# Order of the SyncE transfers where the forward convolution ends and the MLP begins

## The chip, the cores and the metric

One Trainium2 chip, of which one core is used. The metric is the device time of one execution in microseconds (us), the median of the runs. Five engines work side by side: TensorE (PE; PEld is its weight load), VectorE (DVE), ScalarE (ACT), GpSimd (POOL) and SyncE (SP), which here only issues DMA transfers. Each engine works through its own list of instructions in order. Transfers move data between the chip's DRAM and its on-chip memory on 16 DMA engines, which SP's and POOL's transfers share.

## The reference

Four residual layers on x of shape 2048 x 512 (bf16), convolution and MLP in turn, and the gradients of all inputs and weights for a given `grad_out`:

```
x = x + A(layernorm(x))        # A(q) = q * (conv(kv, ssm_k) + kv * ssm_D),  kv = shift_conv(k) * v
x = x + B(layernorm(x))        # B(x) = gelu(x w1 + b1) w2 + b2,  w1 512 x 1376
x = x + A(layernorm(x))
x = x + B(layernorm(x))
outputs: x, and d/d(q, k, v, shift_k, ssm_k, ssm_D, w1, b1, w2, b2) of <x, grad_out>
```

The bracket in A does not depend on x, so the kernel computes it once, as `y`, and uses it in both A layers. The long convolution is done by a real Fourier transform of length 4096, as matmuls with tables of cosines and sines.

## The kernel before, in words

`ssm_kernel` runs three stages: `phase_conv_forward` (which makes y), `phase_mlp` (all four layers forward, and the backward pass of the MLPs) and the backward convolution together with the weight gradients. The change is at the end of the first stage and at the start of the second.

**End of the forward convolution.** The spectrum is cut into five groups, 0 to 4. For each group `spectrum(g)` is TensorE's transform of kv, evicted by ScalarE into a tile `KVg`; `multiply(g)` is VectorE's product of `KVg` with the spectrum of the filter (tiles `pr_t`, `pr_u`, result `Yg`, or `y_res` for group 3); `inverse(g)` is TensorE's back transform (`iv_ps`), evicted by ScalarE into `W[m]`, m = 0, 1. The filter's spectrum lies in DRAM (`Hspec_d`); `load_spec(g)` fetches a group of it. Groups 2 and 4 share one buffer, `Hg`, so `load_spec(4)` waits until `multiply(2)` has read it for the last time; `multiply(4)` waits for `load_spec(4)`. `store_spec(g)` writes `KVg` to DRAM for the backward stage.

In the same stretch q is normalised for the first layer. Its four slices of 512 rows, `qs[0]` to `qs[3]`, lie in the memory that the MLP weights take over afterwards: slices 0 and 1 under `w1`, slices 2 and 3 under `w2` (both have the name `w_sb` in the profile). When a slice is normalised, POOL stores it to DRAM (`n_d<-w_sb`). `start_weights(..., 0)` loads w1 and `start_weights(..., 1)` loads w2 (rows 0 to 1279, then the last 96) and the bias b2 as one more row of w2's tile. So a weight's load waits for POOL's stores out of the memory that it overwrites. `load_x(s)` brings slice s of the residual x into `x_sl` by two transfers, and `y_res<-n_d` brings normalised slices 0 and 1 back.

After `multiply(4)` VectorE runs `even()` (tiles `ib` and `W`), then `res.w.finish()`, one small instruction that scales the row b2 (`w_sb<-w_sb`), then `block0` (`ibx`, `W`, `y_res`), which gives the first rows of y, and `first_sum`, the first residual sum with its statistics (`rstd`, `nmr`). From these ScalarE makes the normalised rows for the first MLP (`low<-x_sl,nmr,rstd`), SP turns them by DMA transposes (`low<-low`), and TensorE multiplies them with w1 (`mm_ps<-low,w_sb`). Before that TensorE makes turned copies of both weights (`oo_ps<-ident,w_sb`, `oo_ps<-w_centre,w_sb`, evicted into `w2T_sb` and `w1T_sb`); the very first of these reads the last chunk of w2, with the scaled row b2 in it. VectorE meanwhile works through the rest of the back transform (`others`, `outs`) and the sums of the next rows, and blocks of 256 rows follow one another through both MLPs.

**What sets the order.** In the convolution each engine's list is the order in which the code calls its operations. In the MLP it is the list of numbers `SEQUENCE`, by which `Plan.listed` takes the planned steps. `flip_rows` copies `grad_out` with rows of each second half block reversed from DRAM to DRAM (`goB_d`, 1024 rows of 1 KB); it is read much later by the backward pass of the MLP.

Of the kernel before, what the change touches and what calls it, by code (L numbers as in the profile page):

```python
# [195 lines left out]
def flip_rows(out, src2d, first, eng, n=256):  # L196
    rs = src2d.ap[0][0]
    eng.dma_start(out=out, in_=bass.AP(tensor=src2d.tensor, offset=src2d.offset + first * rs,
                                           ap=[[512 * rs, out.shape[0]], [-rs, n], [1, src2d.shape[1]]]))
# [8 lines left out]
def tok_io(nc, sb, ap2d, flipped, i, store=False, eng=None):  # L208
    eng = eng or nc.sync
    lo = ap2d[i * 512:i * 512 + 256, :].rearrange("(t p) d -> p t d", p=P)  # L210
    hi = flipped[i].rearrange("(t p) d -> p t d", p=P)
    for s, d in ((sb[:, 0:2, :], lo), (sb[:, 2:4, :], hi)):
        last = eng.dma_start(out=d, in_=s) if store else eng.dma_start(out=s, in_=d)
    return last
# [628 lines left out]
def phase_conv_forward(ctx, nc, tc, dims, consts, dram, res, aps):  # L843
# [4 lines left out]
    nc = Ordered(nc, tc, ("tensor", "vector", "scalar", "gpsimd", "sync"))  # L848
# [26 lines left out]
    order = p.listed(OPEN_SEQUENCE, start, dict(OPEN_FREE))  # L875
    b_ = Slots(Ordered(nc.nc, tc, ("tensor", "vector", "scalar", "gpsimd", "sync")), tiles, p.held, None)
# [45 lines left out]
    def store_spec(g):  # L922
        lo, src = (0, KVpair[0]) if g == 1 else (GROUPS[g][1], KVs[g])
        nc.sync.dma_start(out=dram.KVspec[:, :, lo:lo + 4, :], in_=src)

    def load_x(s):
        tok_io(nc, res.x[:, s * TS:(s + 1) * TS, :], aps["A_q"].flatten_outer_dims(), dram.qB, s)
# [37 lines left out]
    for g in (3, 4):  # L965
        sts.append(fk.streams(GROUPS[g][0], spare[g - 3]))
    tmp = [foldp.tile([P, 2, 2, 2, 512], BF16, name=f"ib{x}", tag=("fold_s", "fold_d")[x], bufs=1) for x in range(2)]
    start_weights(nc, res.w, dims, aps, 0)
    res.x = res.xpool.tile([P, NT, D], BF16, name="x_sl", tag="fold_x", bufs=1)
    spectrum(3, lambda: normalise("scalar"))  # L970
    multiply(2)
    load_spec(4)
    load_x(0)
    nc.sync.dma_start(out=ns[0], in_=tok(dram.n[0], 0))
    store_spec(3)
    spectrum(4, lambda: normalise("scalar"))
    res.low = [shared(res, "low", i) for i in range(len(SHARED))]
    load_x(1)
    nc.sync.dma_start(out=ns[1], in_=tok(dram.n[0], 1))
    start_weights(nc, res.w, dims, aps, 1)  # L980
    store_spec(4)
    for s in (2, 3):
        load_x(s)
    inverse(2)
    multiply(3)
    inverse(3)
# [3 lines left out]
    for m in range(2):  # L990
        ib[m].even()
    res.w.finish()
    flip_rows(dram.goB, aps["grad_out"].flatten_outer_dims(), 511, nc.sync)
    inverse(4)
    yv = res.y[:, :, :].rearrange("p (i h) d -> p i h d", i=4)
    px = foldp.tile([P, 2, 2, 2, 512], BF16, name="ibx", tag="fold_t", bufs=2)
# [330 lines left out]
def start_weights(nc, w, dims, aps, part):  # L1327
    D, F, ND, NFC = dims.D, dims.F, dims.ND, dims.NFC
    FP = NFC * P
    nfull = F // P  # L1330
    rem = F - nfull * P
    assert rem == 96
    w1_ap, w2_ap = aps["B_w1"], aps["B_w2"]
    if part == 0:
        nc.sync.dma_start(out=w.w1[:, :, 0:F], in_=w1_ap.rearrange("(c p) f -> p c f", p=P))
        nc.gpsimd.memset(w.w1[:, :, F:FP], 0.0)
        nc.gpsimd.memset(w.centre, -1.0 / D)
        return
    nc.gpsimd.memset(w.w2[rem:P, nfull, :], 0.0)
    nc.sync.dma_start(out=w.w2[:, 0:nfull, :], in_=w2_ap[0:nfull * P, :].rearrange("(c p) d -> p c d", p=P))  # L1340
    nc.sync.dma_start(out=w.w2[0:rem, nfull, :], in_=w2_ap[nfull * P:F, :])
    nc.sync.dma_start(out=w.w2[rem:rem + 1, nfull, :], in_=aps["B_b2"].rearrange("(o d) -> o d", o=1))

    def finish():
        b2 = w.w2[rem:rem + 1, nfull, :]
        nc.vector.tensor_scalar(out=b2, in0=b2, scalar1=1.0 / PAD_H, scalar2=None, op0=ALU.mult)

    w.finish = finish
# [6 lines left out]
def tok(ap2d, s):  # L1355
    return ap2d[s * 512:(s + 1) * 512, :].rearrange("(t p) d -> p t d", p=P)
# [822 lines left out]
LATE = {}  # L2179
SEAM = 9.0  # L2180
READY = {0: -5.0, 1: 0.5, 2: -5.0, 3: -5.0, -1: -12.0, -2: -12.0}
FREE = {"PE": -12.0, "ACT": -10.8, "DVE": -3.4, "POOL": 0.4, "SP": -10.0}
SEQUENCE = (
# [132 lines left out]
@with_exitstack  # L2316
def phase_mlp(ctx, nc, tc, dims, consts, dram, res, aps):
    S, D, F, NT, ND, NFC = dims.S, dims.D, dims.F, dims.NT, dims.ND, dims.NFC
    go_ap = aps["grad_out"].flatten_outer_dims()
    out0 = aps["out_0"].flatten_outer_dims()  # L2320
    out1 = aps["out_1"].flatten_outer_dims()
    m = Mid()
    m.D, m.ND, m.NFC = D, ND, NFC
    m.sum_on_act = False
    m.ident, m.ones_f = consts.ident, consts.onescol_f
    m.x, m.y, m.rstd, m.nmr, m.mhalf = res.x, res.y, res.rstd, res.nmr, res.mhalf
    m.st, m.mv, m.tail = res.st, res.mv, res.tail
    m.n_d, m.h_d, m.gz_d, m.gp_d = dram.n, dram.h, dram.gz, dram.gp
    with ExitStack() as st:
        lanes = st.enter_context(tc.tile_pool(name="m_l", bufs=1, reuse_waits="tile"))  # L2330
        psum = st.enter_context(tc.tile_pool(name="m_ps", bufs=1, space=bass.MemoryType.PSUM, reuse_waits="tile"))
        m.w = res.w
        w, tiles = m.w, {k: [] for k in SIZES}

        w.w2T = lanes.tile([P, ND, NFC * P], BF16, name="w2T_sb")
        w.w1T = lanes.tile([P, NFC, D], BF16, name="w1T_sb")
        low = [res.low[i][:, x * 1024:x * 1024 + 1024] for i in (1, 2, 3) for x in range(2)]
        tiles["n"], tiles["nT"] = low[0:4], low[4:6]

        def slots(tag, n):  # L2340
            for _ in range(n):
                i = len(tiles[tag])
                tiles[tag].append(lanes.tile([P, SIZES[tag]], BF16, name=f"l_{tag}_{i}"))

        for tag, k in (("g", 4), ("h", 1), ("n", 4), ("u", 2)):
            slots(tag, k)
        big, small, rest = [], [], []
        for t in res.old:
            k = t.shape[-1] // 4096
            big += [t[:, 2816 * i:2816 * i + 2816] for i in range(k)]  # L2350
            small += [t[:, 2816 * k + 1024 * i:2816 * k + 1024 * i + 1024] for i in range(k)]
            rest.append(t[:, 3840 * k:4096 * k])
        tiles["g"] += big[0:4]
        tiles["h"] += [big[7]] + big[4:7]
        tiles["nT"] += [*small[0:2], small[7]]
        tiles["gx"], tiles["g1"] = small[2:6], [small[6]]
        junk = [rest[1]]
        tiles["dg"] = [rest[3 + i // 2][:, P * (i % 2):P * (i % 2) + P] for i in range(4)]
        m.cols = rest[2].bitcast(F32).rearrange("p (a t) -> p a t", a=8)
        w.b1col = rest[5][:, 0:2 * NFC].bitcast(F32)  # L2360
        tiles["mm"] = [psum.tile([P, 512], F32, name=f"mm_ps{i}") for i in range(SLOTS["mm"])]
        tiles["oo"] = [psum.tile([P, 512], F32, name=f"oo_ps{i}") for i in range(SLOTS["oo"])]

        def forward_done(b_):
            res.wstack.close()
            gp_ = res.gystack.enter_context(tc.tile_pool(name="gres", bufs=1, side="right"))
            G3 = gp_.tile([P, NT, D], BF16, name="G3")
            gypool = res.gystack.enter_context(tc.tile_pool(name="gypool", bufs=1, side="right"))
            m.gy = res.gy_bf = gypool.tile([P, NT, D], BF16, name="gy_bf")
            m.G = [G3, res.x]  # L2370

        p = Plan(SLOTS)

        def load_g(b_, x):
            s, e = x // 2, x % 2
            src = dram.goB[s] if e else go_ap[s * 512:s * 512 + HB, :]
            b_.nc.sync.dma_start(out=m.G[0][:, 2 * x:2 * x + 2, :], in_=src.rearrange("(t p) d -> p t d", p=P))

        m.early, m.behind = {}, []

        def early(b_, k):
            m.early[k] = shared(res, "dw_tm", k)[:, :].rearrange("p (t f) -> p t f", t=NT)
            which, i, c = weight_grad_units(NFC)[k]
            b_.nc.sync.dma_start_transpose(out=m.early[k], in_=m.h_d[(3, 1)[i]][:, c, :])

        p = mlp_plan(m, consts, dram, go_ap, out0, out1, aps["B_b1"], forward_done, load_g, early)
        order = p.listed(SEQUENCE, lambda o: READY.get(o.blk, 1.0), dict(FREE))
        b_ = Slots(Ordered(nc, tc, ("tensor", "vector", "scalar", "gpsimd", "sync")), tiles, p.held, junk)
        fill = busy_fill(order, p.held)
        for o in order:  # L2390
            if o in fill:
                (tag, i), n = fill[o]
                keep_busy(b_.nc, consts, tiles[tag][i][:, 0:256], n)
            o.fn(b_)
    return m


# [63 lines left out]
```

## Time and profile before

| | |
|---|---|
| median of 3 runs | 772.45 us (771.81, 772.45, 776.12) |
| profiled execution, its own time | 779.16 us |
| its span | 777.4 us |
| TensorE, VectorE, ScalarE, GpSimd busy | 95%, 92%, 75%, 30% of the span |
| granted clock of TensorE, mean | 0.993 |
| DMA, mean over the span | 220 GB/s |

The profile is of one execution, whose time stands beside its span. Its times are counted from the start of the span. The page gives each engine's busy time and the chain of work that ended last; the queries used here are the waits (who waited for whom), the timeline (instructions of one engine in order of time, neighbours of one kind merged), the windows (busy time, granted clock and DMA traffic of a stretch) and the DMA issues with their time to landing. The change moves transfers that are issued between 108 and 156 us of the span.

### The profile page before, as it was taken

Reading aid. Unit: us, or ns where it says so; the run is one execution under the profiler, and the core shown is the slowest. Engines: PE = TensorE matmul, PEld = TensorE weight load, DVE = VectorE, ACT = ScalarE, POOL = GpSimd, SP = SyncE. Lnnn points to the kernel's source line nnn. Section 1 sums busy time; section 2 is a strip of 40 time slices with the busy share of each in tenths; the row PEclk is TensorE's granted clock in tenths of the full one; section 3 lists DMA queues with packets and bytes.
Section 4 is the critical chain, followed back from the end, with each engine's and each line's share of the span. In section 5 each row is a group of like instructions: output and inputs, shape, how many; then the busy total and the mean of one; then the engine's idle time right before and its main releaser. Section 6 shows DMA issues by size and latency. Waiting matters only on the chain. (4 is left out here: it accounts for less than half of the span.)

```text
span 777.4 us, 13662 instructions
## 1 busy us (share of the span) xinstructions
PE 740.9 (95%) x5167; PEld 453.5 (58%) x5167; DVE 713.4 (92%) x1154; ACT 580.7 (75%) x788; POOL 234.8 (30%) x308
## 2 busy tenths in 40 slices
PE   8999897879999999999999999989999999999996
PEld 6765343566566666767566566534444456567764
DVE  8997987899999999999999998993999998999972
ACT  5999895689999999999888865445323169986761
POOL 4534960002224426434425342220012223020110
PEclk9999999999999999999999999999999999999998
DMA  9878769614655457569779879999999997844561
GB/s 316 313 287 310 268 234 379 139 41 141 174 160 146 123 134 202 181 170 256 179 217 257 216 205 232 217 251 323 264 274 261 318 369 259 312 113 168 160 183 44
DMA packets 205528, 170.96 MB, mean 220 GB/s; under 512 B 100435, under 2 KB 185110, under 8 KB 205334
## 3 DMA queue, kind: packets, MB, share of 16 engines
q1 hardware_dynamic: 192246, 128.88, 59.9%
q0 software_dynamic: 13216, 41.20, 14.6%
q8 instruction: 40, 0.66, 0.3%
q14 instruction: 26, 0.21, 0.1%
HBM read 76.36 MB, written 76.36 MB: 196 GB/s over the span
## 5 line engine op out<-in xcount | busy, mean ns | idle before, releaser
L56 PEld LDWEIGHTS <-w_sb 128*128 128x128 bf16 x903 | 85.9, 99 | 39.8 <-DMA low<-low 5.2
L56 PEld LDWEIGHTS <-dw_tm 128*128 128x128 bf16 x672 | 63.3, 98 | 64.1 <-issue 0.3
L56 PE MATMUL mm_ps<-low,w_sb 128*128 128x256 bf16 x660 | 88.3, 276 | 3.7 <-DMA low<-low 3.7
L56 PE MATMUL dw_ps<-G,dw_tm 128*128 128x512 bf16 x336 | 83.1, 379 | 0.0
L56 PE MATMUL dw_ps<-x_sl,dw_tm 128*128 128x512 bf16 x336 | 80.2, 379 | 0.0
L56 PEld LDWEIGHTS <-w2T_sb 128*128 128x128 bf16 x704 | 68.8, 98 | 16.4 <-issue 1.0
L56 POOL TENSOR_TENSOR rstd<-rstd,mhalf 128x2 f32<-128x2 f32 (+1 forms) x28 | 36.3, 1296 | 104.8 <-DVE rstd L56 103.5
L56 POOL TENSOR_SCALAR ibx<-ident,ib 128x128 bf16<-128x128 bf16 x32 | 33.4, 1044 | 84.5 <-DVE W L56 82.1
L56 PE MATMUL mm_ps<-W,w2T_sb 128*128 128x256 bf16 x440 | 58.3, 272 | 0.5 <-ACT l_g L56 0.3
L56 ACT ACTIVATE l_g<-l_g 128x2816 bf16<-128x2816 bf16 x22 | 57.3, 2604 | 1.4 <-DVE l_g L56 1.2
L2149 ACT ACTIVATE dw_o<-dw_ps 128x512 bf16<-128x512 f32 x21 | 12.5, 594 | 49.9 <-PE dw_ps L56 38.1
L2039 ACT ACTIVATE dw_tm<-dw_tp 128x1024 bf16<-128x1024 bf16 x38 | 38.9, 1024 | 9.9 <-PE dw_tp L56 9.5
L56 DVE SCALAR_TENSOR_TENSOR gw_junk<-gy_bf,kTc 128x1024 bf16<-128x1024 bf16 x32 | 39.2, 1225 | 2.9 <-ACT gy_bf L1176 1.3
L56 PEld LDWEIGHTS <-ib 128*128 128x128 bf16 x264 | 25.6, 98 | 27.8 <-DVE ib L56 1.0
L56 ACT ACTIVATE l_n<-l_n,ib 128x512 bf16<-128x512 bf16 x32 | 25.5, 828 | 13.5 <-POOL ib L56 8.2
L56 PE MATMUL oo_ps<-w1T_sb,ib 128*128 128x512 bf16 x154 | 35.0, 379 | 0.0
L56 ACT ACTIVATE low<-x_sl,nmr,rstd 128x512 bf16<-128x512 bf16 x36 | 30.3, 873 | 5.4 <-DVE nmr L56 5.4
L56 PE MATMUL mm_ps<-lane_t,w2T_sb 128*128 128x256 bf16 x264 | 34.0, 273 | 0.0
L56 ACT ACTIVATE W<-W 128x2816 bf16<-128x2816 bf16 x12 | 31.8, 2647 | 0.0
L56 ACT ACTIVATE ibx<-mm_ps 128x512 bf16<-128x512 f32 (+1 forms) x36 | 20.4, 580 | 14.2 <-PE mm_ps L56 14.1
L56 DVE TENSOR_TENSOR l_g<-l_g,l_g 128x2816 bf16<-128x2816 bf16 x19 | 30.7, 1613 | 0.0
L56 PE MATMUL oo_ps<-w_sb,l_h 128*128 128x512 bf16 x132 | 30.4, 379 | 0.0
(381 smaller groups left out, 1973.7 us busy)
## 6 DMA issues: line engine op xcount, KB each, us to landing
dw_fm<-gz_d SPq DMA_DIRECT2D x22, 512.0 KB, 8.8
l_n<-n_d SPq DMA_DIRECT2D x26, 256.0 KB, 4.1
gz_d<-ib SPq DMA_DIRECT2D x7, 704.0 KB, 5.1
W<-gp_d SPq DMA_DIRECT2D x7, 704.0 KB
n_d<-low SPq DMA_DIRECT2D x18, 256.0 KB, 2.6
h_d<-l_h SPq DMA_DIRECT2D x6, 704.0 KB
gz_d<-ibx SPq DMA_DIRECT2D x6, 704.0 KB, 4.4
KVspec_d<-KVg SPq DMA_DIRECT2D x4, 1024.0 KB
```

The costliest lines, as they stand in the source:

```text
L56: return self.tc.keep_in_program_order(f(*args, **kwargs))
L2039: nc.scalar.activation(out=dst, in_=ps, func=ACT.Identity)
L2149: nc.scalar.activation(out=o, in_=ps, func=ACT.Identity)
```

## The change

Nothing is added to the computation and nothing is left out; SP issues the same transfers in another order. The load of w1 moves behind `load_spec(4)`, the first slice of x and the first normalised slice; the loads of x slices 2 and 3 move ahead of w2; b2 is issued ahead of w2 instead of behind it; and the flipped copy of `grad_out` is issued inside the MLP, after the eighth of SP's planned steps, instead of ahead of the MLP.

```diff
@@ phase_conv_forward
-    start_weights(nc, res.w, dims, aps, 0)
     res.x = res.xpool.tile([P, NT, D], BF16, name="x_sl", tag="fold_x", bufs=1)
     spectrum(3, lambda: normalise("scalar"))
     multiply(2)
     load_spec(4)
     load_x(0)
     nc.sync.dma_start(out=ns[0], in_=tok(dram.n[0], 0))
+    start_weights(nc, res.w, dims, aps, 0)
     store_spec(3)
     spectrum(4, lambda: normalise("scalar"))
     res.low = [shared(res, "low", i) for i in range(len(SHARED))]
     load_x(1)
     nc.sync.dma_start(out=ns[1], in_=tok(dram.n[0], 1))
+    for s in (2, 3):
+        load_x(s)
     start_weights(nc, res.w, dims, aps, 1)
     store_spec(4)
-    for s in (2, 3):
-        load_x(s)
     inverse(2)
...
     res.w.finish()
-    flip_rows(dram.goB, aps["grad_out"].flatten_outer_dims(), 511, nc.sync)
     inverse(4)
@@ start_weights, part 1
     nc.gpsimd.memset(w.w2[rem:P, nfull, :], 0.0)
+    nc.sync.dma_start(out=w.w2[rem:rem + 1, nfull, :], in_=aps["B_b2"].rearrange("(o d) -> o d", o=1))
     nc.sync.dma_start(out=w.w2[:, 0:nfull, :], in_=w2_ap[0:nfull * P, :].rearrange("(c p) d -> p c d", p=P))
     nc.sync.dma_start(out=w.w2[0:rem, nfull, :], in_=w2_ap[nfull * P:F, :])
-    nc.sync.dma_start(out=w.w2[rem:rem + 1, nfull, :], in_=aps["B_b2"].rearrange("(o d) -> o d", o=1))
@@ phase_mlp
+FLIP_AFTER = 7
...
+        flip_after = [o for o in order if o.eng == "SP"][FLIP_AFTER]
         for o in order:
...
             o.fn(b_)
+            if o is flip_after:
+                flip_rows(dram.goB, go_ap, 511, b_.nc.sync)
```

The lists of TensorE, VectorE and ScalarE stay as they were; SP's changes at three places, and on POOL the third store of a normalised slice now stands ahead of the clearing of w1's spare columns.

The first place is SP's list where `multiply(2)` ends. Before (`w_sb<-in_B_w_dram 128x4x1376` is w1, `Hg` the spectrum of group 4):

```order
L56 DMA KVspec_d<-KVg 256x1x2048
L56 DMA w_sb<-in_B_w_dram 128x4x1376
L56 DMA Hg_1482<-Hspec_d 128x2x2048
L56 DMA x_sl<-in_A_q_dram 128x2x512
L56 DMA x_sl<-qB_d 128x2x512
L56 DMA y_res<-n_d 128x4x512
```

and now:

```order
L56 DMA KVspec_d<-KVg 256x1x2048
L56 DMA Hg_1479<-Hspec_d 128x2x2048
L56 DMA x_sl<-in_A_q_dram 128x2x512
L56 DMA x_sl<-qB_d 128x2x512
L56 DMA y_res<-n_d 128x4x512
L56 DMA w_sb<-in_B_w_dram 128x4x1376
```

w1 went from ahead of these four loads to behind them.

The second place is SP's list around w2 (`w_sb<-in_B_w_dram 128x10x512` and `96x512`; `w_sb<-in_B_b_dram` is b2). Before, from the second normalised slice on:

```order
L56 DMA y_res<-n_d 128x4x512
L56 DMA w_sb<-in_B_w_dram 128x10x512
L56 DMA w_sb<-in_B_w_dram 96x512
L56 DMA w_sb<-in_B_b_dram 1x512
L56 DMA KVspec_d<-KVg 256x1x2048
L56 DMA x_sl<-in_A_q_dram 128x2x512
L56 DMA x_sl<-qB_d 128x2x512
...
L56 DMA low<-in_B_b_dram 1x5x128 x2
```

and now:

```order
L56 DMA y_res<-n_d 128x4x512
L56 DMA x_sl<-in_A_q_dram 128x2x512
L56 DMA x_sl<-qB_d 128x2x512
...
L56 DMA w_sb<-in_B_b_dram 1x512
L56 DMA w_sb<-in_B_w_dram 128x10x512
L56 DMA w_sb<-in_B_w_dram 96x512
L56 DMA KVspec_d<-KVg 256x1x2048
L56 DMA low<-in_B_b_dram 1x5x128 x2
```

The four loads of x slices 2 and 3 went ahead of w2, and b2 stands first of the three.

The third place is SP's list at the start of the MLP. Before:

```order
L56 DMA low<-in_B_b_dram 1x96
L56 DMA goB_d<-in_grad_out_dram 1024x1x512
L56 DMA_TRANSPOSE low<-low 128x4x128 x2
L56 DMA low<-n_d 128x2x512 x2
L56 DMA_TRANSPOSE lane_t<-in_grad_out_dram 128x4x128
```

and now:

```order
L56 DMA low<-in_B_b_dram 1x96
L56 DMA_TRANSPOSE low<-low 128x4x128 x2
L56 DMA low<-n_d 128x2x512 x2
L56 DMA_TRANSPOSE lane_t<-in_grad_out_dram 128x4x128
L56 DMA_TRANSPOSE low<-low 128x4x128 x2
L56 DMA_TRANSPOSE lane_t<-in_grad_out_dram 128x4x128
L56 DMA goB_d<-in_grad_out_dram 1024x1x512
```

The flipped copy went from ahead of the first block's transposes to behind the second pair of them.

## Rows read from the trace of the kernel before

**Rows 1.** The chain that ended last, its first piece: start us, us, what

```profile
481.28 0.36 DVE x_sl L56
```

**Rows 2.** Waits of VectorE, 100 to 175 us: total us, times, longest us

```profile
DVE pr_t L56 <- DMA Hg<-Hspec_d: 6.6, 1, 6.6
DVE nmr L56 <- POOL rstd L56: 1.7, 2, 0.9
```

**Rows 3.** Timeline of VectorE: start us, us, instruction, count [idle before, who ended it]

```profile
104.70 1.28 DVE L56 TENSOR_TENSOR pr_u<-KVg,Hg 128x1024 bf16<-128x1024 bf16 x2
...
113.60 0.68 DVE L56 TENSOR_TENSOR y_res<-pr_u 128x1024 bf16<-128x1024 bf16 x1
120.92 1.22 DVE L56 TENSOR_TENSOR pr_t<-KVg,Hg 128x2048 bf16<-128x2048 bf16 x1 [6.64 <-DMA Hg<-Hspec_d]
...
135.71 0.29 DVE L56 TENSOR_SCALAR w_sb<-w_sb 1x512 bf16<-1x512 bf16 x1
...
168.43 0.15 DVE L56 SCALAR_TENSOR_TENSOR nmr<-ln_mvs,rstd 128x2 f32<-128x2 f32 x1
```

**Rows 4.** Timeline of SP's queue, its issues: start us, us, transfer

```profile
108.34 0.38 SPq L56 DMA_DIRECT2D w_sb<-in_B_w_dram  x1
108.88 0.57 SPq L56 DMA_DIRECT2D Hg<-Hspec_d  x1
...
130.26 0.71 SPq L56 DMA_DIRECT2D x_sl<-qB_d  x1
...
136.16 0.72 SPq L56 DMA_DIRECT2D goB_d<-in_grad_out_dram  x1
145.88 2.64 SPq L56 DMA_TRANSPOSE low<-low  x2
...
154.00 1.27 SPq L56 DMA_TRANSPOSE lane_t<-in_grad_out_dram  x1
...
170.17 2.50 SPq L56 DMA_TRANSPOSE low<-low  x2
```

**Rows 5.** Waits of SP's queue, 94 to 150 us

```profile
SPq L56 <- DMA n_d<-w_sb: 14.4, 3, 11.4
```

**Rows 6.** Windows: stretch, length, busy (count) by engine, TensorE's clock, DMA share, GB/s

```profile
108.00:109.00 1.00, 1.00 (x7) 0.43 (x5) 1.00 (x3) 1.00 (x2) 0.61 (x2) 1.00 0.00 0
...
110.00:137.00 27.00, 22.78 (x113) 10.51 (x112) 19.99 (x28) 16.95 (x25) 3.18 (x7) 1.00 1.04 371
...
138.00:147.00 9.00, 7.57 (x62) 4.44 (x60) 7.64 (x16) 5.93 (x11) 0.72 (x1) 1.00 0.28 90
...
174.00:178.00 4.00, 4.00 (x20) 2.71 (x21) 3.93 (x9) 3.97 (x2) 1.26 (x1) 0.57 0.90 252
```

**Rows 7.** DMA issues near 103, 109, 113, 130, 172 us: KB each, us to landing

```profile
n_d<-w_sb POOLq DMA_DIRECT2D x2, 512.0 KB, 3.9
...
n_d<-w_sb POOLq DMA_DIRECT2D x1, 512.0 KB, 10.2
...
n_d<-w_sb POOLq DMA_DIRECT2D x1, 512.0 KB, 8.3
...
x_sl<-qB_d SPq DMA_DIRECT2D x2, 256.0 KB, 8.8
...
ib<-in_grad_out_dram SPq DMA_DIRECT2D x1, 256.0 KB, 3.0
```

**Rows 8.** Timeline of TensorE, instructions that waited

```profile
127.54 3.18 PE L56 MATMUL iv_ps<-Yg,vt 128*128 128x512 bf16 x14 [2.45 <-DVE Yg L56]
...
136.06 0.68 PE L56 MATMUL oo_ps<-ident,w_sb 128*128 128x128 bf16 x9 [1.77 <-DVE w_sb L56]
...
146.39 1.02 PE L56 MATMUL oo_ps<-w_centre,w_sb 128*128 128x512 bf16 x4 [1.43 <-ACT w1T_sb L56]
...
151.56 0.61 PE L56 MATMUL mm_ps<-low,w_sb 128*128 128x256 bf16 x4 [0.81 <-DMA low<-low]
...
173.95 0.61 PE L56 MATMUL mm_ps<-low,w_sb 128*128 128x256 bf16 x4 [2.90 <-DMA low<-low]
```

**Rows 9.** Timeline of ScalarE, its last wait before 200 us

```profile
168.62 1.52 ACT L56 ACTIVATE low<-x_sl,nmr,rstd 128x512 bf16<-128x512 bf16 x2 [2.77 <-DVE nmr L56]
```

## Prediction

> **What bounds the kernel now.** I read the chain that ended last first: it is followed back only to 481 us [rows 1], so it says nothing of the seam, which lies between 100 and 180 us. There the waits decide. VectorE waits twice for something, and only once for long: 6.6 us for the filter spectrum of group 4, `Hg` [rows 2]. The timeline of VectorE shows the place [rows 3]: its work ends at 114.28 (113.60 + 0.68), and `multiply(4)` starts at 120.92. From there to the statistics at 168.43 nothing stops it but 1.7 us of waits for POOL [rows 2]. ScalarE ends its last wait of the seam on just these statistics, at 168.62 after 2.77 us idle [rows 9], and TensorE's wait up to 173.95 ends on the transposes of what ScalarE then makes [rows 8]. So around 170 us both other engines stand behind VectorE, and what VectorE gains before 168 they can gain as well, as long as they arrive no later than it does.
>
> Why `Hg` is late is in SP's queue [rows 4, 5]: SP waits 11.4 us in one piece for POOL's store of a normalised slice, since w1 overwrites it, issues w1 at 108.34, and only then `Hg` at 108.88. The buffer of `Hg` had been free since 105.98, when the second `pr_u` of `multiply(2)` ended (104.70 + 1.28, [rows 3]). And `Hg` then stands behind the 1376 KB of w1. From 110 to 137 us the DMA engines are full, share 1.04 at 371 GB/s; in 108 to 109 they move nothing [rows 6].
>
> **The change part by part.**
>
> *`Hg` ahead of w1.* SP can issue it at about 106.0, when its buffer is free, 2.9 us earlier than before, and with no w1 ahead of it. For its landing I need a rate. From the issue of w1 (108.34) to the landing of the last x load (130.26 + 8.8 = 139.06, [rows 4, 7]) the two queues moved 9920 KB, counted from the shapes: w1 1376, `Hg` 1024, w2 and its rest 1376, two spectrum stores 2048, four x slices 2048, two normalised slices 1024, and POOL's last two stores 1024. A lone 256 KB load lands in 3.0 us [rows 7]; 0.7 of that is its own bytes, so some 2.3 us are fixed, and 9920 KB take 30.72 - 2.3 = 28.4 us, or 349 KB per us. `Hg` issued at 106.0 then lands at 106.0 + 2.3 + 1024/349 = 111.2 if alone; with some 200 KB left of POOL's second store and all 512 KB of its third beside it, at 113.3. VectorE wants it at 114.28. I take the whole 6.64 us as gone; the lower bound is a landing 1 us late, which takes 1 us back.
>
> *What is late next: b2.* VectorE now goes on to `multiply(4)` and `even()`, whose other inputs are there (TensorE starts the back transform of group 4 and waits 2.45 us for VectorE in it, [rows 8]). It reaches `w_sb<-w_sb`, the scaling of b2, at 135.71 - 6.64 = 129.07. Before, it found b2 there. Now b2 stands behind, on SP, 6496 KB: `Hg` 1024, slices 0 to 3 of x 2048, two normalised slices 1024, w1 1376, one spectrum store 1024. With POOL's 1224 KB that is 7720 KB from 106.0 on: b2 lands at 106.0 + 2.3 + 7720/349 = 130.4. So VectorE waits 1.3 us, with everything behind it. Lower bound 0, since one row of 1 KB may not need every queue to be drained; upper bound: b2 lands with the last of the transfers (priced below). I take 1.3, because the landings that the trace shows come in the order of issue (`Hg` at 120.92, the last x load at 139.06).
>
> *w2 behind x.* w2 lands 1280/349 = 3.7 us after b2, its last 96 rows 0.3 later: 134.4. TensorE's wait of 2.45 us in group 4's back transform goes, so it is through with that earlier and waits for w2 until 134.4, where before it waited for the scaled b2 until 136.06 [rows 8]. It starts 1.6 us earlier. Its two further waits up to 151.56, 1.43 us and 0.81 us [rows 8], hang on VectorE's statistics (the `w1T` eviction stands behind the normalised rows in ScalarE's list, and the transposes turn these rows) and go, as the statistics come 5 us earlier; so it reaches the first MLP some 3.8 us earlier. ScalarE's evictions follow TensorE, 3.8 us earlier, and ScalarE has another 2.77 us idle at 168.62 [rows 9]: 6.6 us in all. TensorE has 2.90 us idle at 173.95 [rows 8]: 6.7 us. Both arrive earlier than VectorE's gain asks for, by little more than a microsecond. So VectorE sets the end of the seam.
>
> *The x loads ahead of w2, the first slices ahead of w1.* Their readers (the first sum, at about 135 us now) come long after; I cost them at nothing. Cover: slice 0 stands directly behind `Hg`, some 20 us ahead of its reader.
>
> *The flipped copy.* It takes its bytes slowly: from 138 to 147 us, with hardly anything else to move, the DMA share is 0.28 at 90 GB/s [rows 6], which counts reads and writes as the other rows do, and 1024 KB at that pace take 11 to 12 us. Before, issued at 136.16, it was still running when the first transposes were issued at 145.88 [rows 4], and these landed for TensorE only at 151.56. Now these transposes have the queue to themselves; that gain is inside TensorE's 0.81 us wait above. The copy now starts after the second `lane_t` transpose (154.00 before, some 3 us earlier now, so about 152) and ends near 164. The next transposes, 170.17 before, are due at about 165. I cost it at nothing, covered by a stretch in which the queue is empty, with 1 us to spare; if the cover is gone, TensorE's wait at 173.95 grows by the overlap.
>
> *The clearing of w1's spare columns* on POOL moves behind the third store and nobody waits for it before 131 us: nothing.
>
> *Sum.* 6.64 - 1.3 = 5.3 us. From 170 us on the lists are the same, and each engine waits for the others only, so I carry the shift to the end. The profiled execution would take 779.16 - 5.3 = 773.9 us. It stands 6.7 us above the median of the runs, so from the median: 772.45 - 5.3 = **767.1 us**.
>
> **A rule that speaks against it.** Before, VectorE stands idle for 6.64 us right after POOL issues its fourth store, and that idle time goes. In the rows the store issued at 109 us, under an unbroken run of VectorE, took 10.2 us to land, the one at 113 us, with VectorE idle, 8.3 us, and the first two, also under an unbroken run, a median of 3.9 us [rows 7]; so a busy VectorE alone did not hold a store back, and full DMA engines go with the two long ones. The Trainium skill, page "SBUF — State Buffer", section "SBUF: two separate sides", says that a DMA issued from GpSimd can be starved while VectorE runs in a two-port mode, because its descriptors can't be written. By that rule the fourth store would land only after VectorE's next pause; the first two stores speak against it.
>
> **The rivals.**
>
> 1. *b2 is no hindrance.* It is one row, and may land before 129.07. Then the whole 6.64 us stay: 765.8 us. For it: a wait for it is not in the trace of before; against: it is issued behind 6496 KB on a queue that lands in order. Chance 0.13.
>
> 2. *w2 becomes the bound.* w2 overwrites slices 2 and 3, so SP can't issue it before POOL's fourth store has landed. If VectorE's unbroken run holds that store until VectorE stops at 129.07, it lands at about 129.1 + 3.9 = 133.0, and w2 1376/349 + 2.3 = 6.2 us later, at 139.2. TensorE then starts 3.1 us later than before, gets the 2.2 us of [rows 8] back and is 0.9 us late; of ScalarE's 2.77 us some 1.9 are left as gain: 770.6 us. A milder form has the same end: TensorE waits 3 us for w2, and its clock falls, as it did in 174 to 178 us after the wait of 2.90 (0.57, [rows 6, 8]). Against it: the first two stores [rows 7]. Chance 0.17, the rule above included.
>
> 3. *The copy runs into the transposes.* It ends at 166 or later instead of 164, and the transposes due at 165 queue behind it; 1 to 2 us come back at TensorE's wait: 768.6 us. Chance 0.09.
>
> 4. *Slower: the transfers do not land in the order of issue.* If packets of x, b2, w2 and the last spectrum store are mixed on the engines, b2 lands with the last of them, after 6496 + 1376 + 1024 + 1224 = 10120 KB: 106.0 + 2.3 + 29.0 = 137.3. VectorE then scales b2 1.6 us later than before, and the gain at `Hg` is more than lost: 774.0 us. It decides from a landing after 135.7 on. For it: w2 is now nearly the last of the stream; against: `Hg` landed 18 us ahead of the x loads issued behind it. Chance 0.06.
>
> My forecast has 0.55.
>
> **How the numbers follow.** About 0.5%, here 3.9 us, is what a measurement of this kernel can tell from no change; its three runs lie that far apart. Faster by more: nearly all of the forecast (b2 may land 1.4 us later than I think, 0.48 of 0.55), rival 1 and half of rival 3: 0.66. Within: the rest of the forecast, rival 2, half of rival 3 and rival 4: 0.29. Slower by more needs rival 4 with a second wait: 0.05. The range goes from rival 1 less half a microsecond of scatter, 765.2, to rival 2 with as much on top, 771.1; rival 4 is left out, with the far ends of the others.
>
> **What would show it.** In the profile after: no wait of VectorE for `Hg` near 114 us, or one under 1 us; a wait of about 1.3 us for `w_sb<-in_B_b_dram` at `w_sb<-w_sb`, near 129 to 131 us; TensorE's first `oo_ps<-ident,w_sb` near 134.5, released by w2; ScalarE's `low<-x_sl` of 168.62 near 163.3, still released by VectorE's `nmr`; the copy issued near 152 us, and the transposes of 170.17 near 165 with no longer wait behind them. The forecast is wrong if VectorE waits for b2 past 133 us, if ScalarE's `low` near 163 is held by TensorE or w2, or if the gain at 170 us is there and is smaller at the end.

## The result, and the profile after

| | before | after |
|---|---|---|
| median of 6 runs each | 773.40 us (771.81 to 776.12) | 781.68 us (779.42 to 787.22) |
| ratio of the times, 95% interval | | 1.011, 1.0075 to 1.0146 |
| profiled execution, its own time | 779.16 us | 779.42 us |
| its span, mean granted clock of TensorE | 777.4 us, 0.993 | 777.6 us, 0.988 |

The changed kernel is slower, by 6 to 11 us, where 5.3 us less were forecast. Disturbed runs are left out of every ratio here, while a median is of all runs. The two profiled executions are of the same length all the same. That is the first thing to notice: the execution of before whose rows stand ahead of the prediction took 6 us longer than the median of its kernel, and the one of after did not.

What the change was to do at `Hg`, it does. SyncE's issues after (start us, us, transfer), which answer to [rows 4]:

```profile
104.59 0.57 SPq L56 DMA_DIRECT2D Hg<-Hspec_d  x1
...
107.75 1.36 SPq L56 DMA_DIRECT2D w_sb<-in_B_w_dram  x1
...
142.07 2.63 SPq L56 DMA_TRANSPOSE low<-low  x2
...
152.65 0.76 SPq L56 DMA_DIRECT2D goB_d<-in_grad_out_dram  x1
153.47 7.63 SPq L56 DMA_DIRECT2D n_d<-low  x1
169.37 2.53 SPq L56 DMA_TRANSPOSE low<-low  x2
```

`Hg` is issued first, and VectorE's timeline after has no wait at `multiply(4)` (120.92 in [rows 3]), none for b2 at 127.56, and its statistics come at 160.28 instead of 168.43, 8 us earlier:

```profile
112.77 1.21 DVE L56 TENSOR_TENSOR pr_t<-KVg,Hg 128x2048 bf16<-128x2048 bf16 x1
...
127.56 0.29 DVE L56 TENSOR_SCALAR w_sb<-w_sb 1x512 bf16<-1x512 bf16 x1
...
160.28 0.15 DVE L56 SCALAR_TENSOR_TENSOR nmr<-ln_mvs,rstd 128x2 f32<-128x2 f32 x1
...
175.00 1.62 DVE L56 TENSOR_TENSOR l_h<-W,l_g 128x2816 bf16<-128x2816 bf16 x1 [1.54 <-ACT W L56]
```

Then it is lost within fifteen microseconds: `l_h<-W,l_g`, the last row above, starts at 175.00, against 176.03 in the first profile of before:

```profile
176.03 1.62 DVE L56 TENSOR_TENSOR l_h<-W,l_g 128x2816 bf16<-128x2816 bf16 x1
```

The loss is on ScalarE and TensorE. ScalarE's timeline after, the row that answers to [rows 9], and TensorE's waits after, whose first and last answer to the second and the last of [rows 8]:

```profile
167.83 1.52 ACT L56 ACTIVATE low<-x_sl,nmr,rstd 128x512 bf16<-128x512 bf16 x2 [5.62 <-DMA n_d<-low]
```

```profile
133.03 0.97 PE L56 MATMUL oo_ps<-ident,w_sb 128*128 128x128 bf16 x11 [2.81 <-DMA w_sb<-in_B_w_dram]
...
169.88 0.58 PE L56 MATMUL mm_ps<-low 128*128 128x512 bf16 x1 [3.48 <-ACT l_g L56]
173.19 1.04 PE L56 MATMUL mm_ps<-low,w_sb 128*128 128x256 bf16 x4 [2.73 <-DMA low<-low]
```

ScalarE no longer waits for VectorE's `nmr`, which has been there for 7 us, but for a transfer: the first block's store `n_d<-low`. ScalarE is about to write new rows over that store's source. The store stands right behind the flipped copy in SyncE's queue; its issue alone took 7.63 us. Behind ScalarE TensorE runs dry twice, and its granted clock falls to the lower level (windows after: stretch, length, busy by engine, clock, DMA share, GB/s):

```profile
164.00:168.00 4.00, 2.40 (x22) 1.99 (x21) 3.11 (x7) 0.17 (x1) 0.69 (x1) 1.00 0.19 68
168.00:178.00 10.00, 5.17 (x21) 3.14 (x22) 3.85 (x6) 9.97 (x8) 0.00 (x0) 0.53 0.54 152
```

0.53 over ten microseconds is nearly the lower level of 1.2 GHz throughout (0.50), where before it was 0.57 for four [rows 6].

Two questions follow. Is the copy's place the whole of the loss? And why does a profile without the wait for `Hg`, and 8 us ahead of [rows 3] at 160 us, belong to a slower kernel?

### The profile page after: what moved, and what is told of

Read it like the earlier page. It is cut to its first block, busy times and chain, and to the rows that moved or that the text cites. A ratio compares the mean times of both kernels' runs of the same rounds, so it can differ in the third digit from the quotient of the medians.

```text
span 777.6 us, 13585 instructions
## 1 busy us (share of the span) xinstructions
PE 737.1 (95%) x5088; PEld 453.7 (58%) x5167; DVE 712.7 (92%) x1154; ACT 580.8 (75%) x788; POOL 223.0 (29%) x308
## 5 line engine op out<-in xcount | busy, mean ns | idle before, releaser
L56 PE MATMUL dw_ps<-G,dw_tm 128*128 128x512 bf16 x319 | 79.9, 379 | 0.8
L56 PE MATMUL dw_ps<-x_sl,dw_tm 128*128 128x512 bf16 x326 | 78.5, 379 | 0.6
L56 DVE BATCH_NORM_STATS2 ln_sts<-x_sl 128x6 f32<-128x512 bf16 x44 | 30.0, 681 | 1.4 <-ACT x_sl L56 1.3
```

The costliest lines, as they stand in the source:

```text
L56: return self.tc.keep_in_program_order(f(*args, **kwargs))
```

## The experiments

**e0_after_again** is the changed kernel once more, on the chip of the three runs that follow, without an edit.

> The changed kernel once more, beside the kernel before on the same chip. Theory 1 (the flipped copy stands ahead of the first block's n_d<-low store in SP's queue; ScalarE's next normalised rows overwrite that store's source and wait for it) and theory 2 (w2, now behind the x loads, delays TensorE and all that follows) both expect what was measured, a ratio near 1.011. Theory 3 (the times of the changed kernel scatter for a reason that no profile shows) expects a ratio between 0.995 and 1.015 with a wide interval.

Measured: 778.39 us, ratio 1.0071 (1.0048 to 1.0094). Slower again. ScalarE is idle for 5.41 us at the same place; its timeline puts that down to `ln_sts` of VectorE, which was long done by then, so the name is of no weight here:

```profile
167.34 1.52 ACT L56 ACTIVATE low<-x_sl,nmr,rstd 128x512 bf16<-128x512 bf16 x2 [5.41 <-DVE ln_sts L56]
```

**e1_flip_back** keeps the new order of the loads and puts the copy back ahead of the MLP.

```diff
     res.w.finish()
+    flip_rows(dram.goB, aps["grad_out"].flatten_outer_dims(), 511, nc.sync)
...
-            if o is flip_after:
-                flip_rows(dram.goB, go_ap, 511, b_.nc.sync)
```

> The changed order of the loads, with the flipped copy at its old place ahead of the MLP. Theory 1: VectorE's 6.6 us stay, ScalarE's wait for n_d<-low near 162 us is gone, ratio 0.991 to 0.994 (5 to 7 us faster than before). Theory 2: as slow as the changed kernel, ratio 1.005 to 1.015, and no wait for n_d<-low to explain it. Theory 3: no forecast below 0.995.

Measured: 773.99 us, ratio 1.0004 (0.9978 to 1.0031); its profiled execution took 771.40 us. ScalarE's wait is gone:

```profile
162.10 1.57 ACT L56 ACTIVATE low<-x_sl,nmr,rstd 128x512 bf16<-128x512 bf16 x2
```

So the copy's place makes the loss. But with the loss undone the kernel is as fast as before, not faster: the gain at `Hg` is in the profile and not in the median.

**e2_flip_on_pool** issues the same copy at the same step from GpSimd's queue.

```diff
-                flip_rows(dram.goB, go_ap, 511, b_.nc.sync)
+                flip_rows(dram.goB, go_ap, 511, b_.nc.gpsimd)
```

> The changed kernel with the flipped copy issued at the same moment, but from POOL's queue instead of SP's. Theory 1: the store n_d<-low no longer stands behind the copy, it lands within 3 to 6 us of its issue, ScalarE's wait is gone, ratio 0.991 to 0.995. If the copy holds the store because both use the same DMA engines, and not because both are in SP's queue, the wait stays at 3 us or more. Theory 2: ratio 1.005 to 1.015.

Measured: 781.85 us, ratio 1.0099 (1.0074 to 1.0124). It does not help, but what it shows is another collision. GpSimd's list was not held up at this step as SyncE's was, so the copy went out 12 us earlier, and the first block's transposes on SyncE's queue had to wait for it (the issue on GpSimd's timeline, then TensorE's wait):

```profile
140.62 1.71 POOL L56 DMA_DIRECT2D goB_d<-in_grad_out_dram  x1
```

```profile
153.14 1.04 PE L56 MATMUL mm_ps<-low,w_sb 128*128 128x256 bf16 x4 [6.79 <-DMA low<-low]
```

A second queue gave the transposes no protection from the copy. Whether the queue or the DMA engines hold the store, e2 does not answer: the copy landed 15.9 us after its issue, near 156.5, and the store went out only at 156.88.

**e3_flip_after_store** lets the store go first and the copy directly behind it.

```diff
-FLIP_AFTER = 7
+FLIP_AFTER = 8
```

> The changed kernel with FLIP_AFTER = 8: the copy is issued directly behind the first block's n_d<-low store instead of ahead of it. Theory 1: ScalarE's wait for n_d<-low is gone; the copy still runs to about 166 us, so the second block's transposes, issued near 163, queue behind it and TensorE waits 2 to 5 us for low<-low; ratio 0.993 to 0.998, between the changed kernel and e1. Theory 2: ratio 1.005 to 1.015.

Measured: 773.96 us, ratio 1.0016 (0.9996 to 1.0036). One place further in the queue takes ScalarE's wait away: the store's issue falls from 7.63 to 1.50 us, and ScalarE goes on at 160.41 without a wait (SyncE's and ScalarE's timelines):

```profile
151.07 1.50 SPq L56 DMA_DIRECT2D n_d<-low  x1
152.61 0.76 SPq L56 DMA_DIRECT2D goB_d<-in_grad_out_dram  x1
```

```profile
160.41 1.59 ACT L56 ACTIVATE low<-x_sl,nmr,rstd 128x512 bf16<-128x512 bf16 x2
```

Again it is no faster than before, where a ratio of 0.993 to 0.998 was expected. What the expectation named at TensorE is there: the second block's transposes now run into the copy, and TensorE waits for them (its timeline), where in e4 below it waits 0.77 us.

```profile
168.31 0.61 PE L56 MATMUL mm_ps<-low,w_sb 128*128 128x256 bf16 x4 [3.28 <-DMA low<-low]
```

VectorE, 1.5 us ahead of e4 at 170 us, is 1.1 us behind it at 192 us. The profiled execution of e3 took 778.79 us, 4.8 us above its own median: at 600 us it is 2 us ahead of e4, and from there to 660 us it has waits for transfers `dw_fm<-gz_d`, 3.7 us in one piece at TensorE, which e4's profile has not.

What is open now is the kernel before itself.

**e4_before_again** is the kernel before, without an edit, for a second profile of it.

> The kernel before, once more, for a second profiled execution of it: the first (779.16 us) lies 6 us above the median of its runs. Theory A: the 6 us are a delay that only some executions have, somewhere else in the program; then this one, at about 773 us, still shows VectorE's wait of 6 to 7 us for Hg near 114 us, and its instructions run ahead of the first profile's from one other place on. Theory B (rival): the wait for Hg is itself what varies; then an execution of 773 us shows it at 0 to 2 us, VectorE is some 6 us ahead of the first profile from 121 us on, and there was little for the change to take away. Theory C: the 6 us are spread over many small waits; then the difference grows slowly, by under 1 us in any 20 us.

Measured: 773.85 us, ratio 1.0006 (0.9974 to 1.0038); the profiled execution took 773.68 us. Theory B held as to the time: there was little to take away. VectorE goes into `multiply(4)` without any wait, and SyncE issues w1 at 101.62, where it stood at 108.34 in [rows 4] (VectorE's, then SyncE's timeline of e4):

```profile
113.58 1.21 DVE L56 TENSOR_TENSOR pr_t<-KVg,Hg 128x2048 bf16<-128x2048 bf16 x1
```

```profile
101.62 0.38 SPq L56 DMA_DIRECT2D w_sb<-in_B_w_dram  x1
105.39 0.57 SPq L56 DMA_DIRECT2D Hg<-Hspec_d  x1
```

Why w1 was late in the first profile is on GpSimd, one step further back than the prediction went. Its timeline in the first profile of before:

```profile
86.80 15.53 POOL L56 TENSOR_TENSOR nmr<-q_mv,rstd 128x4 f32<-128x4 f32 x1
102.41 0.73 POOL L56 TENSOR_SCALAR nmr<-nmr 128x4 f32<-128x4 f32 x1
103.09 1.60 POOL L56 DMA_DIRECT2D n_d<-w_sb  x2
```

and in e4:

```profile
86.17 1.26 POOL L56 TENSOR_TENSOR nmr<-q_mv,rstd 128x4 f32<-128x4 f32 x1
87.52 0.28 POOL L56 TENSOR_SCALAR nmr<-nmr 128x4 f32<-128x4 f32 x1
87.97 0.84 POOL L56 DMA_DIRECT2D n_d<-w_sb  x1 [0.18 <-issue]
```

A product of 128 x 4 numbers took 15.53 us in that one execution; in the other twelve profiled executions here it took 0.20 to 1.26 us. Three times earlier in the same execution it took 0.20 to 0.99 us. It held back the first two stores of normalised slices by 15 and 9 us, these held back w1, and w1 held back `Hg`. e6 below, with the same order of the loads, has no wait for `Hg` either.

**e5_hg_only** is before with w1's load alone moved behind `Hg`.

```diff
-    start_weights(nc, res.w, dims, aps, 0)
...
     nc.sync.dma_start(out=ns[0], in_=tok(dram.n[0], 0))
+    start_weights(nc, res.w, dims, aps, 0)
```

> The kernel before with one part of the change alone: w1's load stands behind Hg's, the n_d load and all else as before (x loads behind w2, b2 last, flipped copy ahead of the MLP). If VectorE's wait for Hg is on the path of typical executions: the wait goes, VectorE is 5 to 7 us ahead at 121 us and at 180 us, and the median falls by 4 to 6 us, to 767 to 769. If it is not (theory B above, or the gain is waited away after 200 us): VectorE is ahead at 121 us by less, or loses it again, and the median stays within 1.5 us of the kernel before.

Measured: 775.77 us, ratio 1.003 (1.0001 to 1.0059): no gain, if anything a small loss, and more than the 1.5 us that was given for this case. With GpSimd in time, w1 needn't wait; moved behind `Hg` it goes out at 108.63 instead of 101.62, all that follows lands later, and b2, still behind w2 here, makes VectorE wait, as the prediction had priced it for the change:

```profile
129.48 0.29 DVE L56 TENSOR_SCALAR w_sb<-w_sb 1x512 bf16<-1x512 bf16 x1 [1.15 <-DMA w_sb<-in_B_b_dram]
```

**e6_flip_alone** is before with the copy alone moved, to the place that the change gives it.

```diff
-    flip_rows(dram.goB, aps["grad_out"].flatten_outer_dims(), 511, nc.sync)
...
+            if o is flip_after:
+                flip_rows(dram.goB, go_ap, 511, b_.nc.sync)
```

> The kernel before with the other part alone: the flipped copy is issued behind the eighth entry of SyncE's list inside the MLP, the loads stand as before. Theory A (the copy's place makes all the loss): the first block's store n_d<-low stands behind the copy, ScalarE waits 4 to 6 us for it ahead of low near 165 us, in place of its 2.77 us for VectorE's nmr; at the end 3 to 6 us slower than the kernel before, about 777 to 779. Rival (the copy harms only together with the earlier seam, since here VectorE is late anyway): ScalarE's wait grows by under 1 us and the median stays within 1.5 us of the kernel before.

Measured: 775.11 us, ratio 1.0049 (1.0022 to 1.0076), a smaller loss than the 777 to 779 us of theory A. The wait is there (waits of ScalarE, 100 to 205 us: total us, times, longest us), and so is the lower clock (windows):

```profile
ACT low L56 <- DMA n_d<-low: 5.0, 1, 5.0
```

```profile
168.00:178.00 10.00, 8.30 (x39) 5.11 (x41) 8.39 (x15) 9.97 (x8) 2.57 (x2) 0.67 0.59 159
```

About 2 us come through at 170 us against 5 to 6 in the changed kernel, because the copy goes out 3 us earlier, at 149.53, and ScalarE goes on 3.7 us earlier, at 164.11: w2 is not behind the x loads here, and TensorE and the transposes before the copy are earlier. In the profiles the two parts of the change are thus worse together than apart: VectorE is 5.3 and 5.8 us behind e4 at 170 us with both, 2.1 with the copy alone and 0.3 with the loads alone (e1). In the times this is not clear, since the intervals of e6 and e0 overlap.

**e7_flip_late** is the changed kernel with the copy twelve of SyncE's steps later.

```diff
-FLIP_AFTER = 7
+FLIP_AFTER = 19
```

> The changed kernel with the flipped copy issued twelve entries of SyncE's list later, behind the transposes of W near 178 us (its first reader on SyncE comes near 211 us). Theory A: nothing near 150 to 175 us stands behind the copy any more, ScalarE has no wait for n_d<-low, and the 6.8 us that VectorE gains at the seam are there at 180 us; some of it is lost again if a transpose or a store after 180 us stands behind the copy; the median is below the kernel before by 0 to 6 us, 767 to 773. Rival (a copy of 12 us on a few of the DMA engines holds whatever follows it, wherever it is put): a new wait of 3 to 6 us at a DMA between 180 and 200 us, and the median at 774 to 779.

Measured: 782.10 us, ratio 1.0117 (1.0082 to 1.0153). The rival held for this place, and worse than it said: up to 178 us next to nothing is lost (`l_h` starts 0.1 us behind e4's), then two stores behind the copy make ScalarE and VectorE wait.

```profile
194.46 2.55 ACT L56 ACTIVATE l_g<-l_g 128x2816 bf16<-128x2816 bf16 x1 [7.24 <-DMA gp_d<-l_g]
```

```profile
195.20 0.69 DVE L56 TENSOR_TENSOR l_n<-l_n,y_res 128x1024 bf16<-128x1024 bf16 x1 [6.29 <-DMA n_d<-l_n]
```

**e8_before_pool_late** and **e9_loads_pool_late** make the accident on purpose, in the kernel before and in e1's order of the loads.

```diff
         if t == TS - 1:
+            for _ in range(28 if s == 0 else 0):
+                nc.gpsimd.memset(res.w.centre, 0.0)
             nc.gpsimd.dma_start(out=tok(dram.n[0], s), in_=qs[s])
```

> The kernel before with GpSimd held up on purpose: 28 clearings of w_centre (0.52 us each, some 14.6 us; it is set to its value afterwards) ahead of its first store of a normalised slice. In the first profile of before GpSimd took 15.53 us over one small operation just there; in the nine other profiled executions it took 0.20 to 1.26 us. Theory (that accident made the wait for Hg): SyncE issues w1 only near 107 to 109 us, VectorE waits 5 to 8 us for Hg near 114, and the median is 4 to 7 us above the kernel before, 777 to 780. Rival (the wait came from something else in that execution): no wait of VectorE for Hg over 2 us, and the median within 1.5 us of the kernel before.

> The changed order of the loads, flipped copy at its old place, and GpSimd held up in the same way. Theory (the order of the loads does what the prediction said, where GpSimd is late): Hg is issued near 106 us all the same, VectorE has no wait for it over 1 us, and the median lies 4 to 7 us below that of the kernel before held up, 771 to 775. Rival (the late stores hold up w1, w2 and TensorE instead): VectorE has no wait for Hg, but TensorE or ScalarE waits longer near 130 to 150 us, and the two held-up kernels end within 2 us of one another.

Measured: GpSimd was held for 16.99 us in both. e8: 779.02 and 780.23 us, the latter with the profile, in its two undisturbed runs, too few for an interval (785.65 us over all four). e9: 773.20 us, ratio to before 1.0002 (0.9972 to 1.0032). The theory held in both, though 1.51 us of wait are left in e9 where under 1 was expected. VectorE's wait for `Hg` in e8, then in e9:

```profile
122.45 1.23 DVE L56 TENSOR_TENSOR pr_t<-KVg,Hg 128x2048 bf16<-128x2048 bf16 x1 [7.20 <-DMA Hg<-Hspec_d]
```

```profile
116.15 1.23 DVE L56 TENSOR_TENSOR pr_t<-KVg,Hg 128x2048 bf16<-128x2048 bf16 x1 [1.51 <-DMA Hg<-Hspec_d]
```

A late GpSimd costs the old order 6 to 7 us against the kernel before beside it (773.04 us), and the new order nothing.

**e10_half_inside** is the changed kernel with half of the copy back at its old place.

```diff
     res.w.finish()
+    flip_rows(dram.goB[:, 0:128, :], aps["grad_out"].flatten_outer_dims(), 511, nc.sync, 128)
...
-                flip_rows(dram.goB, go_ap, 511, b_.nc.sync)
+                flip_rows(dram.goB[:, 128:256, :], go_ap, 383, b_.nc.sync, 128)
```

> The changed kernel with the flipped copy in two halves of 512 KB, the first at the old place ahead of the MLP, the second inside the MLP where the change has the whole. Theory (the store n_d<-low stands behind the copy for as long as the copy runs, and 5.5 us of that show at ScalarE): half the bytes hold it some 6 us less, ScalarE's wait for n_d<-low near 162 to 168 us falls to under 1 us, TensorE's clock stays at 1.00 from 164 to 178 us, and the median falls by 5 to 8 us against the changed kernel, to 771 to 775. Rival (it is not the bytes, but the issue at this place in SyncE's queue that delays the store): the wait stays at 4 to 6 us and the median at 777 to 781.

Measured: 772.59 us, ratio 1.0006 (0.9977 to 1.0035). The theory held: half the bytes at the same place in the queue leave ScalarE no wait, the store's issue takes 1.68 us, and the clock stays up (ScalarE's timeline, windows).

```profile
161.41 1.59 ACT L56 ACTIVATE low<-x_sl,nmr,rstd 128x512 bf16<-128x512 bf16 x2
```

```profile
168.00:178.00 10.00, 9.69 (x63) 5.87 (x62) 9.53 (x13) 9.97 (x11) 2.44 (x2) 1.00 0.52 146
```

All profiles side by side, from two rows of VectorE's timeline in each: the start of `multiply(4)`, the start of `l_h<-W,l_g` behind the stretch in question, and what lies between:

| kernel | copy | wait for `Hg` | `multiply(4)` | `l_h` | between | median |
|---|---|---|---|---|---|---|
| before, first profile | ahead of the MLP | 6.64 | 120.92 | 176.03 | 55.1 | 773.4 |
| e4, before again | ahead of the MLP | 0 | 113.58 | 169.18 | 55.6 | 773.9 |
| e8, before, GpSimd late | ahead of the MLP | 7.20 | 122.45 | 177.56 | 55.1 | two runs near 780 |
| e9, new loads, GpSimd late | ahead of the MLP | 1.51 | 116.15 | 172.10 | 56.0 | 773.2 |
| e1, new loads | ahead of the MLP | 0 | 114.37 | 169.52 | 55.2 | 774.0 |
| e10 | half inside | 0 | 113.44 | 168.68 | 55.2 | 772.6 |
| e3 | behind the store | 0 | 112.38 | 167.68 | 55.3 | 774.0 |
| e5, `Hg` alone | ahead of the MLP | 0 | 113.58 | 171.54 | 58.0 | 775.8 |
| e6, copy alone | inside | 0 | 114.51 | 171.29 | 56.8 | 775.1 |
| after | inside | 0 | 112.77 | 175.00 | 62.2 | 781.7 |
| e0, after again | inside | 0 | 113.91 | 174.52 | 60.6 | 778.4 |
| e2, from GpSimd | inside, 12 us earlier | 0 | 112.33 | 177.24 | 64.9 | 781.9 |
| e7 | inside, behind `l_h` | 0 | 112.65 | 169.32 | 56.7 | 782.1 |

Two separate things move the end: a late GpSimd moves the start of `multiply(4)`, and the copy's place stretches what lies between. The first profile of before had the one, the changed kernel has the other, 5.0 to 6.6 us of it against e4; that is why the two profiled executions came out equal. What is lost behind `l_h` the table does not show: most of e7's loss, and the 2.6 us of e3 above.

No version tried beats the kernel before: e1, e3, e9 and e10 are level with it.

## Why the prediction was wrong

**The step that failed first: "I take the whole 6.64 us as gone".** They do go. But the sum took them as a property of the kernel, and they were one of that execution. The prediction saw its profile stand 6.7 us above the median and noted it as an offset to be carried along ("so from the median: 772.45 - 5.3"), when the wait it was about to remove was 6.64 us long. The two were the same microseconds. It followed the chain from `Hg` to w1 and to POOL's store, named an 11.4 us wait for it [rows 5], and stopped there; one step further back stand the 15.53 us of an operation that took 0.99 us at most at its three earlier places in the same trace. e4 shows the kernel without it, e8 shows that it suffices.

**The second: "I cost it at nothing, covered by a stretch in which the queue is empty".** The copy's pace was right, its end was not: it moves 92 to 98 GB/s, but it ended near 167 us, 14 us after its issue, where about 164 was forecast, so the microsecond to spare before the transposes due at 165 was not there. The windows after show the end:

```profile
161.00:163.00 2.00, 2.00 (x21) 1.73 (x20) 2.00 (x5) 1.21 (x3) 0.00 (x0) 1.00 0.55 195
163.00:166.00 3.00, 3.00 (x30) 2.69 (x28) 2.96 (x5) 0.00 (x0) 0.00 (x0) 1.00 0.27 94
166.00:167.00 1.00, 0.40 (x4) 0.20 (x3) 0.93 (x4) 0.00 (x0) 0.00 (x0) 1.00 0.21 74
167.00:168.00 1.00, 0.00 (x0) 0.00 (x0) 0.18 (x2) 0.17 (x1) 0.69 (x1) 1.00 0.02 7
```

ScalarE was released 15.2 us after the copy's issue. What was overlooked most is the store directly behind it in the queue, and who waits for that: ScalarE overwrites the store's source 9 us later. The prediction asked what the copy would run into among SyncE's transposes, and not which instruction of another engine reuses the memory of a transfer that queues behind. 0 was taken; 5.6 us at ScalarE were measured, and 5.0 to 6.6 us at the end of the stretch, with TensorE's fall to the lower clock in it.

Why a slow copy holds a store is argued, not shown. Where the copy runs alone, the share is 0.27 to 0.28 ([rows 6] and the windows above), that of four or five of the 16 DMA engines. The Trainium skill, page "DMA: Bandwidth & Descriptors", section "Rules for kernel authors", says that a transfer whose outermost dimension has a size below 16 is confined to at most that many engines, and the copy's has four; the trace nearly agrees with it. By the section "Queues, rings and completion order" of that page of the Trainium skill each engine takes the descriptors of one ring in order. A store spread over more engines would then have to wait on those few for the copy. In the windows above about twice the copy's pace moves from 161 to 163 us, just when the store's issue is through (153.47 + 7.63), and ScalarE goes on when the copy has ended; e10, with half the bytes, and e3, with the store in front, agree too. Which engines carried what the trace does not say.

**b2.** 1.3 us were taken, 0 was measured in the changed kernel: it was issued at 123.28 and VectorE never waited. e5, where b2 stands behind w2, has the 1.15 us.

**w2.** TensorE was to start near 134.5, held by w2: 133.03, held by w2 for 2.81 us. Right, and without effect, as the prediction said.

**The rivals.** The first was right in its premise. The third named the copy, but as a collision with transposes, at 1 to 2 us; its condition, an end at 166 us or later, came true, and e3 shows the collision by itself. In the changed kernel the store comes before it, and none of the four had the store. The side on which it came out was given 0.05, nearly all of rival 4's 0.06, though rival 4's own time of 774.0 us lies within the margin called no change. By the Trainium skill, page "SBUF — State Buffer", section "SBUF: two separate sides", GpSimd can't write the descriptors of a transfer while VectorE runs in a two-port mode, which could have held back POOL's fourth store. The trace shows no such hold: that store was issued at 111.59, and w2, which overwrites its source, at 124.00, while VectorE was busy for 11.86 of the 12 us from 112 to 124. Which mode VectorE was in the trace does not say, so the rule itself is not tested here.

**"So I carry the shift to the end".** Held for half of the way: at 435 us what each profile is ahead of or behind e4 at `l_h` is still there within 2 us, e7 excepted, which loses between. At the end of the profiles it is not: e3 goes from 1.5 us ahead to 5.1 us behind, e9 from 2.9 us behind to 0.5 us ahead. Apart from e3's waits behind 600 us that part was not followed up.

## What to carry to other kernels

Before a wait is priced as a gain, ask whether it belongs to the kernel or to the execution that was profiled: if the profile stands above the median by as much as the wait, follow the chain back until the first cause is a normal duration. When a slow transfer moves in a queue, list the transfers behind it, and for each the engine that will next write its source or read its target; an empty stretch of the queue is no cover. A transfer that a few of the DMA engines carry needs a place where the next stores and transposes, here those of some 15 us, have slack, and a second issuing queue does not make one.

## What the runs showed that was not expected

One small GpSimd operation took 15.53 us in one profiled execution and at most 1.26 us in the others. What held it is not in the trace and stays open, and so does how often it happens; one profile in the thirteen had it.

A transfer can hold the issuing queue itself: the 256 KB store behind the copy took 7.63 us to issue, and 0.58 us in e4, where the copy was issued 18 us ahead of it.

A short wait can cost clock as well. In the changed kernel TensorE was busy for 2.40 of 4 us in 164 to 168 us and for 0.58 of 4 us up to 172, its granted clock was 0.58 in these last four, and it then ran at 0.50 up to 178 while its waiting work came in; in e4 and e10, with the same work, it stayed at 1.00.
